# Two multiplications by the reciprocal softmax sums, moved from behind the attention visit to later points of the slot

## The chip, the cores and the metric

The kernel runs on one core of a Trainium2 chip. The metric is the device time of one execution in microseconds (us); less is better. Before the change it is 1352.66 us, the median of three runs (1352.47 to 1352.69).

Names of engines: PE is TensorE (matmuls; PEld are its weight loads), DVE is VectorE, ACT is ScalarE, POOL is GpSimd, SP is SyncE, whose queue issues the DMAs.

## What is computed

An attention with normalised queries and keys, followed by a two-layer network. Cut to what matters (8 batches, 12 heads, 448 positions, 64 elements a head; 768 features, 2048 hidden ones; float32 throughout, the two weights as float64 words):

```python
q_n = q / np.sqrt(np.mean(q * q, axis=-1, keepdims=True) + 1e-06) * g_q      # k_n in the same way, with g_k
scores = np.matmul(q_n, k_n.transpose(0, 1, 3, 2)) / np.sqrt(64)
attn = np.exp(scores - np.max(scores, axis=-1, keepdims=True))
attn = attn / (np.sum(attn, axis=-1, keepdims=True) + 1e-09)
x = np.matmul(attn, v).transpose(0, 2, 1, 3).reshape(8 * 448, 768)
h = x @ w_in
out = (h - np.tanh(h)) @ w_out
```

The division by the sum of the exponentials can wait until after the matmul with `v`: the kernel multiplies the result by the sum's reciprocal. The change is about when it does that.

## The kernel before

**Slots and points.** The attention of one batch is done in six *slots*, one for each pair of heads. Slot `s` is batch `b = s // 6`, pair `hp = s % 6`; there are 48. From slot 12 on, `slot(s)` writes one: first the attention's matmuls, then a list `work` of fourteen *points*. The network's matmuls are a generator, `mlp()`. Between two points `run(...)` takes as many matmuls from it as fit in a fifteenth of the slot's time, `gap_ns(s)` times four; a point then issues a few instructions of the attention's preparation for the slots to come. Nobody reorders this later: each engine works through its instructions in the order in which the Python code issues them. The network of earlier batches runs beside the attention of later ones, and after slot 47 it runs alone.

**The visit.** From slot 13 on (`FOLDED`), the attention part is `visit(s, av)`. It interleaves on TensorE the matmuls of the values of slot `s` (L635, and L623 for the last keys) with those of the scores of slot `s + 1` (L569), and takes some 5.7 us in which no matmul of the network runs. The values go to two banks of PSUM. Then comes `divide(s, av)`: ScalarE copies the first bank to a tile `xT` (L757), VectorE adds the second one (L758), and VectorE multiplies each half of the tile's rows by `rs`, the reciprocal of the sums (two instructions at L762, 64 rows by 448 elements each). After it TensorE computes the third block of the next slot's scores, and then the network goes on.

**The points of a slot**, in order: 1 to 3 add up the next slot's exponentials (`rows`, L600, L606, twice L613); 4 and 5 transpose and reduce them (L710, L717); 6 scales the queries and keys of slot `s + 2` (L530); 7 gathers sums and squares on ScalarE; 8 and 9 transpose queries and keys and sum squares (L540, L544, L508); 10 makes the sums' reciprocals (`spread_sums`, L733 and L734); 11 and 12 are ScalarE's (`weigh_keys`, `meet_blocks`, then `widen_sums`, L741); 13 turns the widened reciprocals into `rs` of slot `s + 1` (`turn_sums`, L747); 14 is empty.

**The network's products.** The hidden layer works by a Strassen-like scheme: seven products in the order 1, 5, 6, 2, 3, 7, 4 (`ORDER`). Each is a chain of matmuls into one of three PSUM banks; products 2, 3 and 7 add to the banks of 1, 5 and 6. After a product VectorE or ScalarE takes the bank's content (an *eviction*: L908 to L924 and L889 for the hidden layer, L1133, L1217, L1223 and L1140 in `project_pair` for the output layer), and the third product after wants the same bank again. In the hidden layer a product is six matmuls, a slot seven products; in `project_pair` a product is four matmuls, and each block of seven is followed by one of eight matmuls of 448 columns (L1126). A matmul of float32 shows as two records.

**x differences.** The Strassen scheme needs differences of x: `x_sums(b, c, ...)` has GpSimd make four of them (L793, 128x224) from the tiles of pairs `c` and `c + 3`. For `c = 0` that is at the fifth point of the slot of pair 4, for `c = 1` at its tenth point, for `c = 2` at the second point of the slot of pair 5. GpSimd also makes the differences of the output layer (`inner_sum`, `u`, L1083), the subtraction of the tanh (L889), and a power for the norms (L523, some 4.8 us, issued by `power_blocks` right behind a visit).

Of the kernel before, what the change touches and what calls it, by code (L numbers as in the profile page):

```python
# [13 lines left out]
ALU = mybir.AluOpType  # L14
# [132 lines left out]
def bounded_path(tc, ctx, q, k, v, moe_w_in, moe_w_out, out, g_col, ident, ones, half_ones, neg_half, early):  # L147
# [17 lines left out]
    nc = tc.nc  # L165
    B, H, S, D = q.shape
# [3 lines left out]
    NP = H // 2  # L170
# [340 lines left out]
    def meet_blocks(s):  # L511

        mine, other = normed["rr", s]
        for g in range(P // BL):
            nc.scalar.copy(out=other[g * BL : (g + 1) * BL], in_=mine[(g ^ 1) * BL : ((g ^ 1) + 1) * BL])
# [32 lines left out]
    def weigh_keys(s):  # L548
        kT = turned[s][1]
        nc.scalar.mul(kT, kT, g_col)  # L550

    def sc_bank():
        return bank_of("sc")

    def scores(s, c, apart=False):

        rr, kT, qT = turned[s]
        n = S if c < KF else HS
        name, bufs = ("p", 2) if c < 2 else ("p_full", 1) if c < KF else ("p_last", 2)
        if c == 1:  # L560
            p = probs[s, 1] = probs[s, 0]
        else:
            p = probs[s, c] = pp.tile([P, 2, 2 if c < 2 else 1, n], F32, name=name, bufs=bufs)
        tiles = [sc_bank() for _ in range(2)]

        def score(h, i):
            at, first = (i * BL, 0) if c < KF else (i * BL % KR, i * BL // KR * n)
            r = slice(h * D, (h + 1) * D)
            nc.tensor.matmul(  # L569
                tiles[h][i * BL : (i + 1) * BL, :n], lhsT=kT[r, c * P + at : c * P + at + BL],  # L570
                rhs=qT[r, first : first + n], start=True, stop=True,
            )

        def exp(h):
            nc.scalar.activation(  # L575
                p[:, h, c if c < 2 else 0, :], tiles[h][:, :n], AF.Exp,
                scale=1.0 if rr is None else rr[:, 0, 2 * c + h : 2 * c + h + 1],
            )

        if apart:  # L580
            return [(lambda i, h=h: score(h, i), lambda h=h: exp(h)) for h in range(2)]
        for i in range(P // BL):
            for h in range(2):
                score(h, i)
        for h in range(2):
            exp(h)
# [5 lines left out]
    def add(s, now=True):  # L592

        if s <= NP + NP // 2:
            sums[s] = []
            return
        t = early["sum"]
        sums[s] = [t]
        p = full(s)
        nc.vector.tensor_tensor(out=t, in0=p[0], in1=p[1], op=ALU.add)  # L600
        if now:
            add_third(s)
# [126 lines left out]
    def spread_sums(s):  # L729

        acc = whole[s]
        total = whole[s] = late["blocks"].tile([2 * BL, NJ], F32, name="sum_all")
        nc.vector.reduce_sum(total, acc.rearrange("p g j -> p j g"), axis=AX.X)  # L733
        nc.vector.reciprocal(total, total)  # L734

    def widen_sums(s):

        total = whole[s]
        room = late["blocks"].tile([P, 2 * S], F32, name="sum_T")
        wide = whole[s] = room[: 2 * BL, :S].rearrange("p (j k) -> p j k", k=BL)  # L740
        nc.scalar.copy(out=wide, in_=total[:, :, None].to_broadcast([2 * BL, NJ, BL]))  # L741
# [7 lines left out]
    def divide(s, av):  # L749
        b, hp = steps[s]  # L750
        rs = whole.pop(s)
        if b > PAIRED and b % 2 and hp == 1:
            x = xT[b, hp] = late["blocks"].tile([P, S], F32, name="xT_more", bufs=1)
        else:
            x = xT[b, hp] = xp.tile([P, S], F32, name="xT")
        if s >= FOLDED:
            nc.scalar.copy(out=x, in_=av[0][:, :S])  # L757
            nc.vector.tensor_tensor(out=x, in0=x, in1=av[1][:, :S], op=ALU.add)  # L758
        for m in range(2):
            rows = slice(m * D, (m + 1) * D)  # L760
            if s >= FOLDED:
                nc.vector.tensor_tensor(out=x[rows], in0=x[rows], in1=rs, op=ALU.mult)  # L762
                continue
            for n in range(2):
                nc.vector.tensor_tensor(
                    out=x[rows, n * HS : (n + 1) * HS], in0=av[n][rows, :HS], in1=rs[n * D : (n + 1) * D],
                    op=ALU.mult,
                )
        for c in range(NCH):
            del probs[s, c]  # L770
        if b < PAIRED and hp >= HC:
            c = hp - HC
            x_sums(b, (c,), range(4), nc.vector if b == 0 and c == HC - 1 else nc.gpsimd)

    def x_sums_later(s, second):
        b, hp = steps[s]
        for c in {(HC + 1, 1): (0,), (HC + 1, 2): (1,), (HC + 2, 0): (2,)}.get((hp, second), ()):
            x_sums(b, (c,), range(4), nc.gpsimd)

    def x_sums(b, chunks, which, eng):  # L780

        for c in chunks:
            x11, x12, x21, x22 = (xT[b, r][:, n : n + HS] for r in (c, c + HC) for n in (0, HS))
            for i in which:
                if i != 2 and (b, i) not in tt:
                    tt[b, i] = tp.tile([P, HC, HS], F32, name=f"tt{i}", bufs=1)
                out, a, z = (
                    lambda: (tt[b, 0][:, c], x12, x11),
                    lambda: (tt[b, 1][:, c], x22, tt[b, 0][:, c]),
                    lambda: (x12, x22, x12),  # L790
                    lambda: (tt[b, 3][:, c], x21, tt[b, 1][:, c]),
                )[i]()
                eng.tensor_tensor(out=out, in0=a, in1=z, op=ALU.subtract)  # L793


    late = {}
# [579 lines left out]
    def gap_ns(s):  # L1376

        if s < 2 * NP:
            return H_NS / 12 if s % NP < 3 else 4 * S / ENGINE_NS * CD * CF / 12
        if s < 3 * NP:  # L1380
            return (H_NS + O_NS + AHEAD_NS) / (4 * NP)
        n = (s - 3 * NP) % (2 * NP)
        return (H_NS / 16, OUTER_NS * SOON / 8, H_NS / 16, OUTER_NS * (len(OUTER) - SOON) / 8)[(n > 3) + (n > 5) + (n > 9)]

    def has(s):
        return 0 <= s < NS

    def first_slot(s):
# [31 lines left out]
        if has(s):  # L1420
            divide(s, av)
# [34 lines left out]
    def slot(s):  # L1456

        gap = gap_ns(s)
        av = av_banks
        if has(s + 1):  # L1460
            scores(s + 1, KF)
        if s < FOLDED:
            last_values(s, av)
            totals(s, sc_bank())
            divide(s, values(s, av))
            for c in range(KF):
                scores(s + 1, c)
        else:
            visit(s, av)
        if has(s + 2):  # L1470
            load(s + 2, "v")
        rows, ahead, following = has(s + 2), has(s + 3), has(s + 1)
        folded = following and s + 1 >= FOLDED
        first = s + 3 == TURNED
        scaled = rows and not first
        if scaled:
            power_blocks(s + 2)
        work = (
            (
                (following, lambda: add(s + 1, False)), (first, lambda: turn(s + 2, sc_bank(), sc_bank())),  # L1480
                (ahead and not first, lambda: load_blocks(s + 3)),
            ),
            (
                (following, lambda: add_third(s + 1)), (first, lambda: load_blocks(s + 3)),
                (True, lambda: x_sums_later(s, 0)),
            ),
            ((following, lambda: add_last(s + 1)),),
            ((folded, lambda: fold(s + 1)),),
            ((folded, lambda: fold_rest(s + 1)), (True, lambda: x_sums_later(s, 1))),
            ((scaled, lambda: scale_blocks(s + 2)),),  # L1490
            ((folded, lambda: gather(s + 1, 0)), (ahead, lambda: square_blocks(s + 3))),
            ((scaled, lambda: turn_blocks(s + 2, 0)), (folded, lambda: gather(s + 1, 1))),
            ((scaled, lambda: turn_blocks(s + 2, 1)), (ahead, lambda: norm_blocks(s + 3))),
            ((folded, lambda: spread_sums(s + 1)), (True, lambda: x_sums_later(s, 2))),
            ((scaled, lambda: weigh_keys(s + 2)), (ahead, lambda: meet_blocks(s + 3))),
            ((folded, lambda: widen_sums(s + 1)),),
            ((folded, lambda: turn_sums(s + 1)),),
            (),
        )
        for point in work:  # L1500
            run(4 * gap / (len(work) + 1))
            for wanted, fn in point:
                if wanted:
                    fn()
        run(4 * gap / (len(work) + 1))
# [10 lines left out]
    for s in range(2 * NP, NS):  # L1516
        slot(s)
# [346 lines left out]
```

## Time and profile before

| what | value |
|---|---|
| median of the three runs | 1352.66 us |
| the profiled execution | 1352.3 us |
| its span, first to last instruction | 1350.5 us |
| TensorE's mean granted clock | 0.997 |
| busy: PE, PEld | 1317.8, 1032.7 us |
| busy: DVE, ACT, POOL | 952.5, 566.3, 772.5 us |
| L762, x 64 (and 6 to `xT_more`) | median 619 ns, at most 1595 ns |
| L758, x 32 (and 3 to `xT_more`) | median 621 ns |
| L793 on POOL | median 659 ns, at most 1507 ns |

The share of busy time is an average over stages that differ: up to about 300 us the weights are converted, from there to about 1190 us attention and network run side by side, and then the network runs alone. "Idle before, releaser" is the time an engine stood still before an instruction, and what ended it. The chain of waits is followed back from the last instruction: at each step to whatever released it.

### The profile page before, as it was taken

What the parts mean: (1) busy time and instruction counts of PE and PEld (TensorE: products, weight loads), DVE (VectorE), ACT (ScalarE), POOL (GpSimd) and SP (SyncE); (2) the same over time, 40 slices, a digit from 0 to 9 for tenths busy, and PEclk for the clock granted to TensorE, in tenths of its full rate; (3) what the DMA queues carried; (4) which work ended last, traced back from release to release, by engine and by line L of the source; (5) the groups of instructions that cost most, each with busy time, mean ns of one, the idle gap of its engine ahead of it and who ended that gap; (6) DMA issues with size and microseconds to landing.
All of it is one profiled execution on the core that took longest, in us unless ns stands there. A gap on an engine that the chain in (4) does not pass through costs nothing.

```text
span 1350.5 us, 29252 instructions
## 1 busy us (share of the span) xinstructions
PE 1317.8 (98%) x11352; PEld 1032.7 (76%) x11352; DVE 952.5 (71%) x1401; ACT 566.3 (42%) x1342; POOL 772.5 (57%) x591
## 2 busy tenths in 40 slices
PE   7988999999999999999999999999999999999997
PEld 3467854478998888687788787778777788689986
DVE  4999978766855667587877576768787667533455
ACT  7856654244433454445322346354612254311102
POOL 4766766347846246726698244934599243812661
PEclk9999999999999999999999999999999999999999
DMA  7879879889999766476655867475745765355545
GB/s 172 193 202 267 257 253 252 245 251 282 333 303 269 178 160 175 114 185 149 174 145 136 201 160 177 122 170 163 180 126 150 151 200 158 115 151 175 172 141 102
DMA packets 364743, 253.53 MB, mean 188 GB/s; under 512 B 273012, under 2 KB 303284, under 8 KB 364596
## 3 DMA queue, kind: packets, MB, share of 16 engines
q1 hardware_dynamic: 364592, 251.57, 68.8%
q8 instruction: 92, 1.51, 0.5%
q14 instruction: 55, 0.45, 0.1%
q10 hardware_dynamic: 4, 0.00, 0.0%
HBM read 205.23 MB, written 46.27 MB: 186 GB/s over the span
## 4 chain that ended last, share of the span: by engine, by line
PE 81%; DVE 9%; SPq 3%; DMA 2%; issue 2%; POOL 2%; ACT 0%; DVEq 0%; ACTq 0%; POOLq 0%
PE mm L841 36%; PE mm L1126 23%; PE sc L569 8%; PE sc L635 6%; PE mm L1319 5%; DVE xT L762 1%; DVE rows L613 1%; PE sc L623 1%; DMA gT<-in_moe_w_in_dram 1%; PE sc L673 1%; SPq L289 1%; SPq L127 1%; POOL u L1083 1%; DVE rows L606 1%; DMA w_raw<-in_moe_w_in_dram 1%
## 5 line engine op out<-in xcount | busy, mean ns | idle before, releaser
L841 PE MATMUL mm<-xT,w_f 128*128 128x224 f32 x1296 | 264.0, 353 | 0.6 <-DVE s L912 0.6
L841 PEld LDWEIGHTS mm<-xT,w_f 128*128 128x128 f32 x1296 | 244.5, 190 | 6.3 <-issue 4.1
L569 PE MATMUL sc<-qT,kT 64*32 64x448 f32 (+1 forms) x3072 | 212.7, 498 | 2.3 <-ACT p_last L575 1.3
L841 PE MATMUL mm<-tt,w_f 128*128 128x224 f32 x1044 | 213.6, 356 | 0.6
L841 PEld LDWEIGHTS mm<-tt,w_f 128*128 128x128 f32 x1044 | 195.0, 190 | 18.6 <-issue 15.4
L523 POOL TENSOR_TENSOR rr_mine<-rr_mine,neg_half 128x28 f32<-128x28 f32 x33 | 160.5, 4864 | 2.8
L758 DVE TENSOR_TENSOR xT<-xT,sc 128x448 f32<-128x448 f32 x32 | 19.9, 621 | 178.1 <-PE sc L569 124.1
L1126 PE MATMUL mm<-u,w_f 128*128 128x224 f32 x672 | 136.6, 354 | 1.3 <-DVE sum_all L733 0.9
L889 POOL TENSOR_TENSOR gT<-s,th 128x448 f32<-128x448 f32 x44 | 55.8, 1271 | 142.4 <-ACT th L888 142.4
L1126 PE MATMUL mm<-gT,w_f 128*128 128x224 f32 (+1 forms) x496 | 133.0, 420 | 3.2 <-DVE acc L1133 2.8
L1126 PEld LDWEIGHTS mm<-u,w_f 128*128 128x128 f32 x672 | 126.0, 190 | 8.5 <-POOL u L1083 3.8
L569 PEld LDWEIGHTS sc<-qT,kT 64*32 64x32 f32 x3072 | 70.5, 106 | 69.0 <-issue 51.6
L1126 PEld LDWEIGHTS mm<-gT,w_f 128*128 128x128 f32 x496 | 93.3, 190 | 38.1 <-issue 31.8
L635 PE MATMUL sc<-p,v_nat 64*32 64x448 f32 x1120 | 110.5, 536 | 0.0
L725 ACT COPY sum_g<-sum 32x14 f32<-32x14 f32 x280 | 56.3, 201 | 106.0 <-DVE sum L717 100.3
L1126 PE MATMUL mm<-g,w_f 128*128 128x224 f32 (+1 forms) x360 | 99.5, 428 | 0.0
L575 ACT ACTIVATE p<-sc 128x448 f32<-128x448 f32 x132 | 71.8, 544 | 50.6 <-PE sc L569 36.5
L889 POOL TENSOR_TENSOR g<-s,th 128x448 f32<-128x448 f32 x24 | 30.7, 1280 | 108.2 <-ACT th L888 93.2
L1126 PEld LDWEIGHTS mm<-g,w_f 128*128 128x128 f32 x360 | 67.9, 190 | 27.1 <-issue 26.0
L1319 PE MATMUL mm<-gT,w_out 128*128 128x448 f32 x192 | 74.3, 542 | 0.0
L1083 POOL TENSOR_TENSOR u<-gT 128x448 f32<-128x448 f32 x48 | 59.5, 1260 | 11.1 <-PE mm L1126 11.1
L635 PEld LDWEIGHTS sc<-p,v_nat 64*32 64x32 f32 x1120 | 40.6, 107 | 31.1 <-issue 31.1
(203 smaller groups left out, 2450.0 us busy)
## 6 DMA issues: line engine op xcount, KB each, us to landing
w_f<-w_in SPq DMA_DIRECT2D x196, 384.0 KB, 3.5
w_f<-w_inner SPq DMA_DIRECT2D x63, 512.0 KB, 3.7
w_f<-w_out SPq DMA_DIRECT2D x42, 512.0 KB, 3.9
w_raw<-in_moe_w_out_dram SPq DMA_DIRECT2D x16, 768.0 KB, 5.3
w_in<-w_out SPq DMA_DIRECT2D x21, 384.0 KB, 5.2
qk_nat<-in_q_dram SPq DMA_DIRECT2D x132, 56.0 KB, 2.6
qk_nat<-in_k_dram SPq DMA_DIRECT2D x132, 56.0 KB, 2.3
g<-w_out SPq DMA_DIRECT2D x14, 512.0 KB, 5.4
```

Of the source, the lines that this page charges most:

```text
L127: nc.sync.dma_start(out=last[r * KR : (r + 1) * KR], in_=rest.rearrange("h p d -> p h d"))
L523: nc.gpsimd.tensor_tensor(out=mine, in0=mine, in1=neg_half[:, :1].to_broadcast([P, 2 * NJ]), op=ALU.pow)
L569: nc.tensor.matmul(tiles[h][i * BL : (i + 1) * BL, :n], lhsT=kT[r, c * P + at : c * P + at + BL], rhs=qT[r, first : first + n], start=True ...
L575: nc.scalar.activation(p[:, h, c if c < 2 else 0, :], tiles[h][:, :n], AF.Exp, scale=1.0 if rr is None else rr[:, 0, 2 * c + h : 2 * c + h ...
L635: nc.tensor.matmul(av[g][i * BL : (i + 1) * BL, :S], lhsT=v_nat[keys, h, c, m * BL : (m + 1) * BL], rhs=p[keys, h], start=first, stop=True ...
L725: nc.scalar.copy(out=acc[h * BL : (h + 1) * BL, g], in_=part[g * BL : (g + 1) * BL, h * NJ : (h + 1) * NJ])
L758: nc.vector.tensor_tensor(out=x, in0=x, in1=av[1][:, :S], op=ALU.add)
L841: nc.tensor.matmul(bank[:, f * HS : (f + 1) * HS], lhsT=w[:, c * width + f, :], rhs=moving[p](c), start=(first and f == 0 and c == 0), sto ...
L889: eng.tensor_tensor(out=g[:, rows, cols], in0=h, in1=th, op=ALU.subtract)
L1083: nc.gpsimd.tensor_tensor(out=u[:, half], in0=a[:, half], in1=z[:, half], op=ALU.subtract)
L1126: nc.tensor.matmul(bank[:, :n], lhsT=w(i), rhs=mv, start=(first and i == 0), stop=(i == len(moving) - 1), skip_group_check=not first,)
L1319: nc.tensor.matmul(bank[:, :S], lhsT=w_out_row(f, n // HC)[:, n % HC * P : (n % HC + 1) * P], rhs=g[:, f, :], start=(f == 0), stop=(f == C ...
```

## The change

Three things in the folded slots (13 to 47). The two multiplications are no longer issued behind the add in `divide`; they are put on a list, and the eleventh and the twelfth point issue one each. In a batch's last slot (`hp == 5`) they stay where they were. The differences of `c = 1` go from the tenth point to the fourteenth.

```diff
         if s >= FOLDED:
             nc.scalar.copy(out=x, in_=av[0][:, :S])
             nc.vector.tensor_tensor(out=x, in0=x, in1=av[1][:, :S], op=ALU.add)
+            for m in range(2):
+                rows = x[m * D : (m + 1) * D]
+                late.setdefault("divide", []).append(
+                    lambda rows=rows: nc.vector.tensor_tensor(out=rows, in0=rows, in1=rs, op=ALU.mult)
+                )
         for m in range(2):
             rows = slice(m * D, (m + 1) * D)
             if s >= FOLDED:
-                nc.vector.tensor_tensor(out=x[rows], in0=x[rows], in1=rs, op=ALU.mult)
+                if hp == NP - 1:
+                    divide_rows()
                 continue
...
+    def divide_rows():
+        if late.get("divide"):
+            late["divide"].pop(0)()
...
-            ((folded, lambda: spread_sums(s + 1)), (True, lambda: x_sums_later(s, 2))),
-            ((scaled, lambda: weigh_keys(s + 2)), (ahead, lambda: meet_blocks(s + 3))),
-            ((folded, lambda: widen_sums(s + 1)),),
+            ((folded, lambda: spread_sums(s + 1)),),
+            (
+                (scaled, lambda: weigh_keys(s + 2)), (ahead, lambda: meet_blocks(s + 3)),
+                (True, divide_rows),
+            ),
+            ((folded, lambda: widen_sums(s + 1)), (True, divide_rows)),
             ((folded, lambda: turn_sums(s + 1)),),
-            (),
+            ((True, lambda: x_sums_later(s, 2)),),
```

## The prediction

> **What bounds the kernel now.** I read the page first, then the chain of waits by stretches, then VectorE's and TensorE's timelines around single visits. The page's first part and its chain:
>
> ```profile
> PE 1317.8 (98%) x11352; PEld 1032.7 (76%) x11352; DVE 952.5 (71%) x1401; ACT 566.3 (42%) x1342; POOL 772.5 (57%) x591
> PE 81%; DVE 9%; SPq 3%; DMA 2%; issue 2%; POOL 2%; ACT 0%; DVEq 0%; ACTq 0%; POOLq 0%
> ```
>
> TensorE sets the time, yet 9% of the chain is VectorE, and L762, the line that the change moves, has a share of it. The 98% hides short stops, because a matmul record (352 ns) is longer than the distance from one start to the next (190 ns, the weight load's length). So I looked for starts further apart than that. The slot that begins at 1159 us (number 46 = batch 7, pair 4; s = 6 x batch + pair) has the worst of them. Its TensorE timeline (start, length, then in brackets the idle time before it and who ended it):
>
> ```profile
> 1159.20 1.78 PE L1126 MATMUL mm<-u,w_f 128*128 128x224 f32 x8
> 1160.82 1.68 PE L1126 MATMUL mm<-gT,w_f 128*128 128x224 f32 x8
> 1163.20 1.78 PE L1126 MATMUL mm<-gT,w_f 128*128 128x224 f32 x8 [0.71 <-DVE acc L1133]
> 1165.11 3.27 PE L1126 MATMUL mm<-u,w_f 128*128 128x224 f32 x16
> 1170.08 7.23 PE L1126 MATMUL mm<-gT,w_f 128*128 128x448 f32 x21 [1.70 <-DVE acc L1133]
> ```
>
> TensorE stops for evictions (L1133), and the chain of waits over the same stretch shows why they are late:
>
> ```profile
> 1159.30 0.63 DVE xT L758
> 1159.93 0.02 issue
> 1159.95 1.30 DVE xT L762
> 1161.25 0.03 issue
> 1161.28 1.44 DVE xT L762
> 1162.73 0.03 issue
> 1162.76 0.39 DVE acc L1133
> 1163.15 1.52 DVE rows L600
> ...
> 1169.75 0.29 DVE acc L1133
> 1170.04 0.04 issue
> 1170.08 9.31 PE mm L1126 x32
> ```
>
> VectorE waits for the visit's last matmuls, then adds (L758), multiplies twice (L762), and only then reaches the eviction of a product finished before or during the visit. From there it has no pause until TensorE has stopped three times.
>
> The slots without a stop have a fixed length: L758 starts at 757.77, 779.24 and 800.73, 21.5 us apart. Slot 26 takes 22.64 (617.95 to 640.59). I summed, slot by slot, the part of each start-to-start distance over 0.19 us (0.38 for 448 columns), less the two gaps of 0.09 and 0.10 at a visit's ends that every slot has. In us: s20 0.42, s22 0.87, s23 0.29, s26 1.07, s27 0.69, s28 0.65, s32 0.53, s34 0.86, s35 0.35, s38 1.07, s39 0.64, s40 0.64, s44 0.50, s46 3.30; nothing in the others from s13 on. Together 11.9 us, and every one ends with an eviction by VectorE that comes late in an unbroken row of VectorE work since the visit.
>
> **What the Trainium skill says.** "VectorE: DVE Perf Modes", section on the TRN2 errata, gives an fp32 tensor_tensor (N+151)/0.96 ns: 624 ns for 448 elements. The trace's median for L762 is 619, so it agrees. "SBUF — State Buffer", section "Who interferes with whom", says that a VectorE instruction with two SBUF inputs contends with a GpSimd one that reads SBUF, and the later one blocks. L762 has two SBUF inputs, and the trace agrees in direction: 1.30 and 1.44 us at 1159.95, with GpSimd in its differences (L1083), against 0.62 in quiet slots. "PSUM — Partial Sum Buffer", section "PSUM bank collisions raise a hardware error", tells one to guard a bank by semaphore; here TensorE restarts at 1170.08, 0.05 us after the eviction's end. "Perfetto Trace Analysis", section "Tensor Engine Instruction (MATMUL, LD_WEIGHTS)", says that VectorE is strictly first in, first out, and the whole argument rests on that order.
>
> **The change, part by part.** 35 visits are folded ones (s13 to s47). Six are a batch's last (s17, 23, 29, 35, 41, 47) and keep their place; 29 visits move 58 multiplications. Nothing is added or removed: VectorE's 952.5 us stay, and the instructions moved issue no DMA.
>
> *Taken from behind the visit.* Every VectorE instruction from the visit to the eleventh point comes earlier by 2 x 0.62 = 1.24 us where GpSimd is quiet, by 2.1 (s22, s28) to 2.8 (s46) where it isn't. Where GpSimd is streaming, L600 is next to meet it (1.09 free, 1.60 in s46), so part of the excess comes back there. I count on 1.24 at least less 0.5 of such a shift, 1.24 as the likely value, 2.8 at most. All the sums above but s46's are under 1.24, so they go: 11.24 us in the twelve slots that move (the list without s23 and s35). In s46 I follow the row: without L762, L1133 at 1159.9, L600 to 1161.9, L1133 to 1162.2, L606 (1.7) and L613 (2.0) to 1165.9, transpose to 1167.0, L1133 to 1167.4. TensorE, not stopped before, wants the bank at 1159.3 + 5 x 1.52 = 1166.9; about 0.5 stays. Gain **10.7** of 11.24.
>
> *Put at the eleventh point.* VectorE's order there is row sum and reciprocal (L733, L734), then the first multiplication, then the eviction of product 4 (L924), then the second one, then L747. In slot 27, the one furthest behind, L924 runs at 655.76 and ends at 656.31. It now starts 1.24 earlier and behind one multiplication more, 0.62 to 1.45: between 0.6 earlier and 0.2 later. TensorE writes that bank again three products on (1, 5, then 6), after the visit, at 662.68. That spare of 6.4 us is the cover; without it the price is up to 1.24 us in each of the 20 slots of this kind (s18 to 21, 24 to 27, 30 to 33, 36 to 39, 42 to 45). Cost **0**.
>
> *Put at the twelfth point.* Behind it stands L747, whose result is wanted behind the next visit, or much later now; VectorE idles 3.9 to 8.1 us before L758. Before L747 it also waits 0.2 to 1.2 us for ScalarE's L741, which the second multiplication fills. Cost 0, except in the long slots s28 and s40. There the points are 2.74 us apart. By counting matmuls from gap_ns, the eleventh falls after the first matmul of a product 1, in front of the 1.19 us that VectorE idles before 693.83: free. The twelfth falls at the end of product 5, in front of its eviction (698.17 to 698.55), whose bank TensorE wants at 699.68. Free (0.62) it fits; contended (1.3 to 1.45, and GpSimd streams differences until 701.2) TensorE loses 0.2 to 0.4. I take 0.3 each: **0.6** back.
>
> *The x differences last.* Four GpSimd subtractions (0.66 each, 3.8 us for the four with contention in s28) move from the tenth point to the fourteenth, in six slots. They now follow the multiplication they need by two points, so the wait is met. In s28 and s40 GpSimd does them at 701.15, ten us late already; they now let two inner sums (four L1083) past, which helps those sums if anything. Still ahead of the power that the next slot issues, nothing there is later. Their reader, the next hidden layer, begins at 749. Cost 0; if the cover were gone, 3.8 us in each of the two.
>
> *SP's queue, ScalarE, TensorE's own order.* No instruction of theirs moves. What is late next after VectorE: GpSimd in s27/28, s39/40 and s46 (24.4 us busy of the 25 from 1150), but none of the stops traced back ends with it.
>
> Sum: 10.7 - 0.6 = 10.1. Against the profiled execution: 1352.3 (span 1350.5 and 1.8 around it) becomes 1342.2. The median of the runs is 0.36 above the profiled one: **1342.6**.
>
> **The rivals.** *The lag falls by less.* GpSimd's contention passes whole to L600 and L606, and the row is 0.72 us earlier only (1.24 less 0.52). Then each slot gains the smaller of its sum and 0.72: 7.7, less 1.5 for contended multiplications: 6.2, time 1346.5. For it: L600 took 1.60 and L606 1.72 in s46. Against: in s20 and s32 L600 took its free 1.09 after a slowed L762.
> *GpSimd takes the place of VectorE.* Its sums keep TensorE where it was in s27, 28, 39, 40 and s46; gains stay in s20, 22, 26, 32, 34, 38, 44: 5.3, time 1347.3. For it: GpSimd's busy time there. Against: its sums of 1159.64 to 1165.6 are for the next block.
> *Nothing is gained*, because the stops follow something that moves with the visit; or the order that the compiled program gets is not the one the source says: 1352.
> *Slower.* The eviction of product 4 behind the first multiplication sets TensorE back in the 20 hidden slots, 1.24 each: 24.8 less 11.2 is 13.6, time 1366. It decides from where VectorE reaches that eviction over 6.4 us later than now, or where the bank's next matmul comes before the visit; the records put it after.
>
> **How the numbers follow.** Forecast 0.62, smaller lag 0.14, GpSimd 0.09, no change 0.05, slower 0.10. Less than 0.2% (2.7 us) can't be told from no change. Faster 0.85, same 0.05, slower 0.10. The range goes from all 11.24 us and a little contention saved (1341.0) to beyond the GpSimd case (1348.5); the two last cases, 0.15, are left out.
>
> **What would show it.** Right: TensorE's gaps behind L1133, L912 and L889 gone in the twelve slots, s26 21.5 us long, s23 and s35 as they were; L600 directly behind the add; VectorE's share of the chain lower by about the 1% of L762. The one new gap, if any, is in s28 and s40 before product 3. Wrong: gaps at the same places (the row is not the cause), gaps before a visit (the tail is), or TensorE waiting for L1083.

## The result, and the profile after

Six runs of the changed kernel took 1346.34 us in the median (1344.73 to 1349.41), six of the kernel before 1352.57 (1352.17 to 1352.90). The ratio is 0.9955 with a 95% interval of 0.9945 to 0.9966: 6.2 us less, where 10 were forecast. The profiled execution took 1346.23 us, with a span of 1344.4. Behind the edit all lines stand ten further down: L1133 is now L1143, L1083 is L1093, L889 is L899. The page's first part and its chain:

```profile
PE 1315.8 (98%) x11352; PEld 1035.4 (77%) x11352; DVE 967.6 (72%) x1401; ACT 570.0 (42%) x1342; POOL 789.3 (59%) x591
PE 82%; DVE 5%; POOL 4%; SPq 3%; DMA 3%; issue 2%; ACT 1%; ACTq 0%; DVEq 0%; POOLq 0%
```

(SPq is SP's queue; "issue" is time in which an engine waited for nothing that the profile shows.) VectorE's share of the chain fell from 9% to 5%, where the prediction expected about one point less, and GpSimd's rose from 2% to 4%. Their instruction counts are the same, yet VectorE is busy 15 us longer and GpSimd 17. Single instructions of both take longer where the two work side by side, as the lines below show.

Slot 46 shows what was hoped for and what was left. TensorE's timeline (start, length, and in brackets the idle time and its releaser):

```profile
1155.32 1.78 PE L1136 MATMUL mm<-u,w_f 128*128 128x224 f32 x8
1156.94 3.19 PE L1136 MATMUL mm<-gT,w_f 128*128 128x224 f32 x16
1159.96 3.19 PE L1136 MATMUL mm<-u,w_f 128*128 128x224 f32 x16
1164.10 7.79 PE L1136 MATMUL mm<-gT,w_f 128*128 128x448 f32 x24 [0.94 <-DVE acc L1143]
```

and the chain of waits over it:

```profile
1155.42 0.62 DVE xT L758
1156.04 0.30 DVE acc L1143
1156.34 1.39 DVE rows L600
...
1157.95 1.73 DVE rows L606
1159.68 0.02 issue
1159.71 1.44 DVE rows L613
1161.14 0.03 issue
1161.17 1.46 DVE rows L613
1162.63 0.02 issue
1162.66 1.11 DVE sum_T L710
1163.77 0.29 DVE acc L1143
1164.06 0.04 issue
1164.10 5.91 PE mm L1136 x15
```

The eviction now follows the add at once, and of three stops one is left. The row up to it is shorter by the two multiplications, but what is left of it is slower than it was: L613 takes 1.44 and 1.46 us. In the kernel before it took 0.96 and 0.98:

```profile
1166.64 0.96 DVE rows L613
1167.63 0.98 DVE rows L613
```

It now runs beside GpSimd's differences of the output layer (L1093, 128x448; below they are called inner sums); before, it ran beside the smaller x differences (L793, 128x224). In the quiet slot 30 the two halves take 1.27 us together.

In a slot like 26, where the stops went altogether, L600 follows the add directly:

```profile
617.43 0.62 DVE L758 TENSOR_TENSOR xT<-xT,sc 128x448 f32<-128x448 f32 x1 [3.56 <-PE sc L569]
617.97 1.08 DVE L600 TENSOR_TENSOR rows<-p 128x896 f32<-128x896 f32 x1
```

I took the stops from the distances of TensorE's starts, in the way of the prediction. One table holds the kernel before, the changed one and the experiments told below (us, one profiled execution each, slots with a stop over 0.1 in the first two; "none" leaves the 58 multiplications out, "both" has them in both places, "x last" moves the differences alone, "last" treats the last slots too, "weights" has the other order of loads, "best" puts three edits together):

| slot | before | changed | none | both | x last | last | weights | best |
|---|---|---|---|---|---|---|---|---|
| 20 | 0.42 | 0 | 0 | 0.55 | 0.44 | 0 | 0 | 0 |
| 22 | 0.87 | 0 | 0 | 1.19 | 0.87 | 0 | 0 | 0 |
| 23 | 0.29 | 0.47 | 0.74 | 0.30 | 0.30 | 0 | 0.46 | 0 |
| 26 | 1.07 | 0 | 0 | 1.07 | 1.07 | 0 | 0 | 0 |
| 27 | 0.69 | 0 | 0 | 0.70 | 0.70 | 0 | 0 | 0 |
| 28 | 0.65 | 0.52 | 0 | 1.14 | 0.65 | 0.53 | 0.54 | 0.54 |
| 29 | 0 | 0.45 | 0 | 0.46 | 0 | 0 | 0.46 | 0 |
| 30 | 0 | 0.88 | 0 | 0.76 | 0 | 0.88 | 0 | 0 |
| 32 | 0.53 | 0 | 0 | 0.49 | 0.53 | 0 | 0 | 0 |
| 34 | 0.86 | 0 | 0 | 1.12 | 0.87 | 0 | 0 | 0 |
| 35 | 0.35 | 0.45 | 0.71 | 0.48 | 0.35 | 0 | 0.47 | 0 |
| 38 | 1.07 | 0 | 0 | 1.17 | 1.07 | 0 | 0 | 0 |
| 39 | 0.64 | 0 | 0 | 0.64 | 0.64 | 0 | 0 | 0 |
| 40 | 0.64 | 0.52 | 0 | 1.15 | 0.66 | 0.53 | 0.53 | 0.53 |
| 41 | 0 | 0.46 | 0 | 0.63 | 0 | 0 | 0.47 | 0 |
| 42 | 0 | 0.38 | 0.47 | 0 | 0 | 1.18 | 0 | 0 |
| 44 | 0.50 | 0 | 0 | 0.46 | 0.49 | 0 | 0 | 0 |
| 46 | 3.31 | 1.21 | 1.05 | 5.17 | 3.32 | 1.21 | 1.22 | 0 |
| sum | 11.9 | 5.3 | 3.0 | 17.5 | 12.0 | 4.3 | 4.2 | 1.1 |

From before to changed the sum falls by 6.5 us; the two profiled executions differ by 6.1, and the changed one reached the first visit 0.6 us later (L758 at 307.09, not 306.49), where the code is the same. So the table accounts for the result: the old stops went in nine of the twelve slots, three kept a part or got another one in its place, and four slots that had none have one now.

### The profile page after: what moved, and what is told of

Read it like the earlier page. It is cut to its first block, busy times and chain, and to the rows that moved or that the text cites. A ratio compares the mean times of both kernels' runs of the same rounds, so it can differ in the third digit from the quotient of the medians.

```text
span 1344.4 us, 29274 instructions
## 1 busy us (share of the span) xinstructions
PE 1315.8 (98%) x11352; PEld 1035.4 (77%) x11352; DVE 967.6 (72%) x1401; ACT 570.0 (42%) x1342; POOL 789.3 (59%) x591
## 4 chain that ended last, share of the span: by engine, by line
PE 82%; DVE 5%; POOL 4%; SPq 3%; DMA 3%; issue 2%; ACT 1%; ACTq 0%; DVEq 0%; POOLq 0%
PE mm L851 38%; PE mm L1136 20%; PE sc L569 8%; PE mm L1329 5%; PE sc L635 5%; POOL u L1093 2%; PE sc L673 1%; PE sc L623 1%; POOL rr_mine L523 1%; SPq L965 1%; PE mm L673 1%; SPq L127 1%; DMA w_f<-w_inner 1%; SPq L497 1%; DMA qk_nat<-in_k_dram 1%
## 5 line engine op out<-in xcount | busy, mean ns | idle before, releaser
L758 DVE TENSOR_TENSOR xT<-xT,sc 128x448 f32<-128x448 f32 x32 | 19.9, 621 | 165.1 <-PE sc L569 115.8
L899 POOL TENSOR_TENSOR gT<-s,th 128x448 f32<-128x448 f32 x44 | 57.5, 1308 | 138.0 <-ACT th L898 138.0
L575 ACT ACTIVATE p<-sc 128x448 f32<-128x448 f32 x132 | 71.7, 543 | 50.4 <-PE sc L569 36.0
L899 POOL TENSOR_TENSOR g<-s,th 128x448 f32<-128x448 f32 x24 | 30.3, 1263 | 104.1 <-ACT th L898 104.1
L1093 POOL TENSOR_TENSOR u<-gT 128x448 f32<-128x448 f32 x48 | 63.5, 1344 | 11.1 <-PE mm L1136 11.1
L144 POOL TENSOR_TENSOR rr<-rr,neg_half 112x8 f32<-112x8 f32 (+1 forms) x30 | 49.1, 1664 | 26.7 <-DVE rr L143 26.1
```

Of the source, the lines that this page charges most:

```text
L144: nc.gpsimd.tensor_tensor(out=r, in0=r, in1=neg_half[:rows], op=ALU.pow)
L575: nc.scalar.activation(p[:, h, c if c < 2 else 0, :], tiles[h][:, :n], AF.Exp, scale=1.0 if rr is None else rr[:, 0, 2 * c + h : 2 * c + h ...
L899: eng.tensor_tensor(out=g[:, rows, cols], in0=h, in1=th, op=ALU.subtract)
L1093: nc.gpsimd.tensor_tensor(out=u[:, half], in0=a[:, half], in1=z[:, half], op=ALU.subtract)
```

## The experiments

**The differences alone.** Is anything of this due to the third edit? The kernel before, with that edit only:

```diff
-            ((folded, lambda: spread_sums(s + 1)), (True, lambda: x_sums_later(s, 2))),
+            ((folded, lambda: spread_sums(s + 1)),),
...
-            (),
+            ((True, lambda: x_sums_later(s, 2)),),
```

> Only the x differences go from the tenth to the fourteenth point; the multiplications stay behind the visit. Theory A (the whole gain is VectorE's row behind the visit getting shorter, the differences carry nothing): 1352.6 us, within 1 us of before, TensorE's stops in slots 20, 22, 26, 27, 32, 34, 38, 39, 44 as in before, 0.4 to 1.1 us each. Rival B (the differences' move brings the new stops of slots 28 to 30 and 40 to 42, because GpSimd's sums come in another order against VectorE): these stops, 3.2 us in all, appear here too, with the old ones still there, time 1354 to 1356.

1353.00 against 1352.92, ratio 0.9999 (0.9991 to 1.0008), and the stops of before in every slot (one more, of 0.68 in slot 17, where nothing of the edit is, is not in the table). Moved alone, the differences carry nothing; theory A holds. What their new place does together with the late multiplications was not run.

**Neither place.** What would be left if the multiplications cost nothing anywhere?

```diff
     def divide_rows():
-        if late.get("divide"):
-            late["divide"].pop(0)()
+        fn = late["divide"].pop(0) if late.get("divide") else None
+        return fn
...
                 if hp == NP - 1:
-                    divide_rows()
+                    divide_rows()()
```

> The changed kernel without the 58 multiplications of the 29 slots (the division by the sums is left out there), x differences at the fourteenth point. Theory A (the new stops of slots 28 to 30, 40 to 42 and 46 are other work that stands next in line: GpSimd's sums, SP's queue, the rest of VectorE's row in slot 46): those stops stay, most of them within 0.3 us, and the time is 1345 to 1346.5, as the changed kernel's 1346.3. Rival C (the multiplications cost TensorE 3 to 4 us at their new points): the stops go with them, time about 1342.5.

1344.11 (1342.88 to 1350.19), ratio 0.9945 (0.9929 to 0.9961), which lies between the two theories. The stops of slots 28, 29, 30, 40 and 41 went with the multiplications, against theory A; those of 23, 35, 42 and 46 did not, against rival C. In stops, the new points cost 5.3 - 3.0 = 2.3 us, not the 0.6 of the prediction.

**Both places.** What if the multiplications stand in the old place and in the new one?

```diff
                 if hp == NP - 1:
                     divide_rows()
+                else:
+                    nc.vector.tensor_tensor(out=x[rows], in0=x[rows], in1=rs, op=ALU.mult)
```

> The 58 multiplications stand behind the visit and again at the eleventh and twelfth point (those rows are multiplied by the reciprocal twice). Theory A (the place behind the visit costs 10 us of stops, the later points cost nothing): time of before, 1352.5 within 1 us, with the stops of before. Rival C (the later points cost 3 to 4 us): 1355.5 to 1357, with stops that before does not have, late in the slots.

1357.66 against 1352.92, ratio 1.0036 (1.0023 to 1.0049): 4.7 us over the kernel before. Rival C's time is the nearer one (0.7 above its range), and A's is out; but the stops that were added do not lie late in the slots, as C said: they lie in the row behind the visit (slots 22, 28, 34, 40, 46), in the last slots 29 and 41, and in slot 30. The place behind the visit costs 12.2 us (17.5 less 5.3) with the later one filled, and 8.9 (11.9 less 3.0) without it. The later points cost 5.6 on top of the row behind the visit, and 2.3 alone. Some 1.7 of the 5.6 is a second effect of one long stop: in slot 46 TensorE stood 2.53 us from one start to the next, and then began its next matmuls of 448 columns 0.75 us apart, not 0.38, until 1177.3 us, at a granted clock of 0.51 by the profile. After the 2.06 us of the kernel before the clock stayed at 1.00. The prediction's cost of 0 for the later points comes nearly true in the slots of the hidden layer's first three pairs (18 to 20, 24 to 26 and so on; slot 30 has a cause of its own, told below), and not where GpSimd is busy.

**Which of the new points cost?** One kernel leaves out the multiplications of slots 27 and 39, the other those of 28 and 40. Each ran once (1346.63 and 1343.34 us), so only their traces are read:

```diff
+        if s in (27, 39):
+            late["divide"].clear()
         for m in range(2):
```

> The changed kernel without the four multiplications of slots 27 and 39 (the division is left out for these two pairs of heads). Theory G (these, late in a slot in which GpSimd makes its subtractions and sums, slow GpSimd's unbroken row, and TensorE pays in the middle of the next slot): the stops of slots 28 and 40, 0.52 us each, fall to under 0.1; those of slots 29 and 41 (0.45) stay or fall with them. Rival H (the stop in slot 28 comes from TensorE arriving earlier, whatever the multiplications do): 0.52 stays.

> The changed kernel without the four multiplications of slots 28 and 40 (the division is left out for these two). Theory G: the stops of slots 29 and 41 (0.45 us each), where VectorE's multiplications behind the visit took 2.97 instead of 2.09 us because GpSimd is later, go or fall under 0.1; those of 28 and 40 stay at 0.52, since they come before the eleventh point. Rival H (slot 29's stop is inherited from slot 28's): it stays.

The stops of slots 29 and 41 went in both runs, as theory G says: slot 29 stops only if both sets are there. In slots 28 and 40 a stop of the same size stayed (0.49 us in the first kernel, 0.53 in the second), and by its size H is right. But its place says otherwise. In the changed kernel TensorE stops for GpSimd's inner sums, in the middle of slot 28:

```profile
681.64 2.43 PE L1136 MATMUL mm<-u,w_f 128*128 128x224 f32 x12
684.33 1.02 PE L1136 MATMUL mm<-u,w_f 128*128 128x224 f32 x4 [0.26 <-POOL u L1093]
```

With the multiplications of slot 27 left out, it doesn't stop there but 14 us later, for VectorE. First VectorE's timeline of that kernel (its lines are two further down), then TensorE's:

```profile
694.55 2.02 DVE L1086 TENSOR_TENSOR gT<-gT,g 128x896 f32<-128x896 f32 x1
696.60 1.44 DVE L762 TENSOR_TENSOR xT<-xT,rs_T 64x448 f32<-64x448 f32 x1
698.07 0.69 DVE L1145 TENSOR_TENSOR s<-mm,s 128x224 f32<-128x224 f32 x2
```

```profile
696.62 1.68 PE L1138 MATMUL mm<-g,w_f 128*128 128x224 f32 x8
698.52 1.78 PE L1138 MATMUL mm<-g,w_f 128*128 128x224 f32 x8 [0.23 <-DVE s L1145]
```

This is the stop that the prediction had named: the second multiplication, slowed to 1.44 us, in front of product 5's eviction, and TensorE late at product 3 (0.39 us and 0.10 behind it). In the changed kernel it doesn't show: there TensorE has lost as much already in front of it, and the same multiplication takes the same 1.44 us. Two limits stand side by side in these slots, each worth 0.5 us, and each covers the other: with either set of multiplications left out the other limit's stop is there, and the kernel without any of the 58 is rid of both. The GpSimd one begins in slot 27: there the late multiplications meet GpSimd's subtraction (1.32 us, 1.14 without them), its inner sums come later, and so does the power behind them. GpSimd's lines in the changed kernel, then in the one without the multiplications (the visit's add starts at 660.49 and at 659.73):

```profile
665.70 5.58 POOL L523 TENSOR_TENSOR rr_mine<-rr_mine,neg_half 128x28 f32<-128x28 f32 x1
680.36 3.92 POOL L1093 TENSOR_TENSOR u<-g,u 128x448 f32<-128x448 f32 x2
```

```profile
664.46 4.81 POOL L523 TENSOR_TENSOR rr_mine<-rr_mine,neg_half 128x28 f32<-128x28 f32 x1
677.49 3.92 POOL L1093 TENSOR_TENSOR u<-g,u 128x448 f32<-128x448 f32 x2
```

By the inner sum that TensorE wants (it ends at 684.28, and at 681.41) GpSimd is 2.1 us later against the add.

**The last slots too.** Slots 23, 29, 35 and 41 keep the multiplications behind the visit. Here they go to the seventh and eighth point, the third differences to the ninth:

```diff
             if s >= FOLDED:
-                if hp == NP - 1:
-                    divide_rows()
                 continue
...
-        for c in {(HC + 1, 1): (0,), (HC + 1, 2): (1,), (HC + 2, 0): (2,)}.get((hp, second), ()):
+        for c in {(HC + 1, 1): (0,), (HC + 1, 2): (1,), (HC + 2, 3): (2,)}.get((hp, second), ()):
...
-            ((folded, lambda: gather(s + 1, 0)), (ahead, lambda: square_blocks(s + 3))),
-            ((scaled, lambda: turn_blocks(s + 2, 0)), (folded, lambda: gather(s + 1, 1))),
-            ((scaled, lambda: turn_blocks(s + 2, 1)), (ahead, lambda: norm_blocks(s + 3))),
+            ((folded, lambda: gather(s + 1, 0)), (ahead, lambda: square_blocks(s + 3)), (s % NP == NP - 1, divide_rows)),
+            ((scaled, lambda: turn_blocks(s + 2, 0)), (folded, lambda: gather(s + 1, 1)), (s % NP == NP - 1, divide_rows)),
+            ((scaled, lambda: turn_blocks(s + 2, 1)), (ahead, lambda: norm_blocks(s + 3)), (True, lambda: x_sums_later(s, 3))),
```

> The changed kernel, and in a batch's last slot the multiplications go to the seventh and eighth point and the third differences to the ninth. Theory A (VectorE's row behind the visit makes the stops of slots 23, 29, 35 and 41 too, 0.45 to 0.47 us each): these four go, 1.84 us less than the changed kernel, 1344.5. Rival D (in slots 29 and 41 GpSimd or SP's queue stands next in line, so that the gain there turns into a longer stop in slots 30 and 42): only 0.9 us less, 1345.4, and the stops of slots 30 and 42 grow by about 0.45 each.

1344.92, ratio 0.9947 (0.9935 to 0.9959), 1.4 us under the changed kernel; the interval overlaps the changed kernel's, so the traces decide here. All four stops went, as A says, and slot 42's grew from 0.38 to 1.18, while slot 30's stayed: rival D in one of the two. The stop of slot 29 was a row behind the visit as well: in the changed kernel the two multiplications there take 2.97 us, and took 2.09 before. The lines of the changed kernel, then that of the kernel before:

```profile
708.79 2.97 DVE L762 TENSOR_TENSOR xT<-xT,rs_T 64x448 f32<-64x448 f32 x2
711.79 1.91 DVE L600 TENSOR_TENSOR rows<-p 128x896 f32<-128x896 f32 x1
```

```profile
711.20 2.09 DVE L762 TENSOR_TENSOR xT<-xT,rs_T 64x448 f32<-64x448 f32 x2
```

GpSimd, late from slot 28, ends its inner sums 6.6 us behind the add there, and before 5.7. In both kernels the multiplications run beside them, so the delay fits, but how it makes the multiplications that much longer was not shown.

**The weights in slots 30 and 42.** The stops of slots 30 and 42 end with a DMA, `w_f<-w_in`, not with an engine. SP's timeline of the changed kernel (each row the issues of one kind; lengths are the time to issue):

```profile
748.97 3.48 SPq L965 DMA_DIRECT2D out_dram<-acc  x4
752.55 0.44 SPq L426 DMA_DIRECT2D w_f<-w_in  x1
753.09 2.12 SPq L965 DMA_DIRECT2D out_dram<-acc  x4
755.26 1.03 SPq L117 DMA_DIRECT2D v_nat<-in_v_dram  x2
756.34 2.54 SPq L127 DMA_DIRECT2D v_nat<-in_v_dram  x2
758.93 2.15 SPq L497 DMA_DIRECT2D qk_nat<-in_q_dram  x4
761.13 2.04 SPq L497 DMA_DIRECT2D qk_nat<-in_k_dram  x4
763.27 3.61 SPq L426 DMA_DIRECT2D w_f<-w_in  x6
```

SP issues without a pause, stores and loads of mostly half a microsecond each, and the weights of product 4 (763.27) wait behind eight loads of queries and keys. What counts is the distance from the visit's add to that issue. Over the two slots of six kernels it was 6.13, 6.32, 6.41, 6.66, 6.76 and 6.78 us where there was no stop, and 7.31, 7.32, 7.45, 7.46, 7.74 and 7.96 us where there was one (0.38, 0.47, 0.88, 0.76, 0.88, 1.18). The two single runs fit it too: 0.03 us at 6.94, and 0.33, 0.45 and 0.87 us at 7.45, 7.59 and 7.70. The kernel before stood at 6.66 and 6.32, with little to spare. First I moved the value loads that these slots issue (for slots 32 and 44) to ScalarE's queue; `fetch` takes the queue as a new argument (not shown):

```diff
-                fetch(nc, name, t, src[b, 2 * hp : 2 * hp + 2], in_order(s))
+                fetch(nc, name, t, src[b, 2 * hp : 2 * hp + 2], in_order(s), nc.scalar if s in (32, 44) else None)
```

> The changed kernel; the value loads that slots 30 and 42 issue (four DMAs each) go through ScalarE's queue and not SP's. Theory S (in these slots the network's weights come late because SP's queue is full with issues): the weights are issued some 3.5 us earlier, the stops of slots 30 (0.88) and 42 (0.38) go, time 1.3 us under the changed kernel's, 1345.0. Rival T (the DMA engines themselves are the limit): the stops stay, time unchanged.

1363.11, ratio 1.0071 (1.0057 to 1.0085): the losses in these two slots grew to 8.1 us each, which neither theory had. Of these, some 1.4 us in slot 30 and 1.7 in slot 42 are again matmuls at half the usual rate behind the longest stop. SP's queue stood still for ten us in the middle of its stores. Below are SP's wait from 744 to 760 us (in total, how often, the longest), the stores, and the first moved load on ScalarE's queue:

```profile
SPq L965 <- DMA v_nat<-in_v_dram: 10.2, 1, 10.2
```

```profile
746.44 12.13 SPq L965 DMA_DIRECT2D out_dram<-acc  x4
755.90 0.54 ACT L575 ACTIVATE p_full<-sc 128x448 f32<-128x448 f32 x1
755.95 0.40 ACTq L117 DMA_DIRECT2D v_nat<-in_v_dram  x1
```

The kept trace tells why a store waits for loads of another queue. Each DMA tells of its landing by a semaphore. From 300 us on, the program takes eight semaphores in turn for the DMAs of both queues (in the changed kernel's trace every one of 890 steps goes to the next of the eight), and in 912 pairs whose landing is recorded no DMA is issued before the one ahead of it on its semaphore has landed. The store that stood from 748.04 to 758.26 has the semaphore of the first moved load. On ScalarE's queue that load was issued only at 755.95, between two of its exponentials (L575). A later store started at 762.18, when the fourth moved load, on its semaphore, had landed at 762.16; in slot 42 a store started at 1078.43, the load on its semaphore having landed at 1078.42, and that wait took 8.6 us. So the move tied SP's queue to the point that ScalarE had reached. The run says nothing against theory S and doesn't prove it. So the order was changed instead:

```diff
-                (ahead and not first, lambda: load_blocks(s + 3)),
+                (ahead and not first and s not in (30, 42), lambda: load_blocks(s + 3)),
...
-                (following, lambda: add_third(s + 1)), (first, lambda: load_blocks(s + 3)),
+                (following, lambda: add_third(s + 1)), (ahead and (first or s in (30, 42)), lambda: load_blocks(s + 3)),
```

> The changed kernel; in slots 30 and 42 the loads of queries and keys (eight DMAs on SP's queue) are issued at the second point and not at the first, so that the weights of product 4 are issued before them. Theory S (the stops of slots 30 and 42 are the weights' issue coming 7.3 us and more behind the visit's add, since SP's queue is busy with issues): the weights are issued some 4 us earlier, the stops of 0.88 and 0.38 go, 1345.0 against 1346.3. Rival T (the queries and keys, 0.5 us later, then hold up ScalarE's squares and with them evictions): as long a stop elsewhere in these slots, time unchanged.

1344.92 (1344.25 to 1345.37), ratio 0.9941 (0.9928 to 0.9955), and both stops are gone, with no new one in these slots. The interval touches the changed kernel's; it is the trace that tells the two apart. SP's timeline of this kernel:

```profile
755.71 2.56 SPq L127 DMA_DIRECT2D v_nat<-in_v_dram  x2
758.37 0.54 SPq L426 DMA_DIRECT2D w_f<-w_in  x1
758.95 1.99 SPq L497 DMA_DIRECT2D qk_nat<-in_q_dram  x4
```

Theory S holds: the first of these weights is issued 3.2 and 2.5 us behind the add.

**Together.** A first kernel had the last slots, the value loads on ScalarE's queue, and in slot 46 the last addition, transpose and reduction two points later:

```diff
+        if s == NS - 2:
+            work = list(work)
+            work[2:7] = (), (), work[2], work[3], work[4] + work[6]
```

> The multiplications of a batch's last slots moved too, the value loads of slots 30 and 42 on ScalarE's queue, and in slot 46 the last addition of the exponentials, the transpose and the reduction two points later. If each stop is what it was traced to: slots 23, 29, 35, 41 none, 30 and 42 none, slot 46 from 1.3 to under 0.3, slots 28 and 40 still 0.52: 3.2 us under the kernel with the last slots moved (1344.9), so 1341.7. If SP's queue or VectorE's row is only one of two that stand in line: 1343 to 1344.5.

1360.07, ratio 1.0044 (1.0030 to 1.0058), because of the two long stops (9.3 and 7.1 us) in slots 30 and 42; the stops of slots 46, 23, 29, 35 and 41 went, as expected. With the other order of loads in place of ScalarE's queue:

> The multiplications of the last slots moved too, the weights before queries and keys in slots 30 and 42, and in slot 46 the last addition, transpose and reduction two points later. If the causes are as traced and don't cover one another: stops left only in slots 28 and 40 (0.52 each) and 0.1 in slot 46, 1341.7. If moving them frees a limit behind: up to 1343.5.

1341.92 (1340.97 to 1342.81), ratio 0.9919 (0.9906 to 0.9933). The table's last column is what was expected: 0.54 and 0.53 left in slots 28 and 40, and none in 46. Its interval lies clear below the changed kernel's, and the stops add up: their causes don't cover one another, but for the pair in slots 28 and 40.

## Why the prediction was right, and where its sizes were off

*The row behind the visit* was right, slot by slot: every old stop of slots 20, 22, 26, 27, 32, 34, 38, 39 and 44 went, also the late ones of 27 and 39 just before the next visit. Slot 26 takes 21.57 us now, as long as those without a stop. The gain of 10.7 that the prediction counted for this place is 10.0 of 11.2 in the table (all but slot 46's 1.2; what slots 28 and 40 show now is another stop), and by the stops of all slots the place is worth 8.9 ("before" less "none") or 12.2 ("both" less "changed"), so the way from the multiplications to TensorE's stops is shown. What failed is the count of what stands behind it.

The sum of 10.1 us lost 3.6 in five terms (stops, from the table):

- *Slot 46*, "about 0.5 stays": 1.2 stayed (1.11 up to the eviction and 0.10 behind it). The step took L606 and the two halves of L613 at the lengths they had in the old place, 1.7 and 2.0; L606 kept its 1.7, and beside GpSimd's inner sums the two halves of L613 took 2.9. The rule of the Trainium skill that the prediction used for L762 ("SBUF — State Buffer", section "Who interferes with whom": an instruction of VectorE with two SBUF inputs contends with one of GpSimd that reads SBUF) holds for L613 as well, as 1.44 and 1.46 against 0.63 in a quiet slot show, and I had not carried it on down the row. The page's lock, with the later one blocked, does not describe the lengths: here both sides stretch, GpSimd's L1093 to 1.7 us each, where it takes 1.1 with VectorE idle (at 1152.31). Off by 0.7.
- *The twelfth point in slots 28 and 40*, "I take 0.3 each": 0.49 where it could be seen, and the 0.52 in the changed kernel is GpSimd's, which covers it. Off by 0.4, and by a cause that the sum did not have.
- *Slots 29 and 41*, not in the sum at all: 0.45 and 0.46. The step "what is late next after VectorE" named GpSimd and put it at nothing, since no old stop ended with it. But the multiplications at the late points make GpSimd's row longer, and VectorE's row behind the next visit with it: without those of slots 27 and 39, or of 28 and 40, these two stops are gone. Off by 0.9.
- *Slots 30 and 42*: 0.88 and 0.38. "SP's queue ... No instruction of theirs moves" was true and not enough. SP's queue was full in this stretch and its weights came just in time: the distance from add to issue was 6.66 and 6.32 us before, 7.45 and 7.31 in the changed kernel. It differs from trace to trace (6.13 in slot 30 of "none", 7.32 in slot 42 of the same). Off by 1.3.
- *Slots 23 and 35*, "as they were": 0.18 and 0.10 more. They are VectorE's row, since they go when the multiplications there move; why they grew is open, and not by the late multiplications, since in "none" they are 0.74 and 0.71. Off by 0.3.

The measured 1346.3 is almost the 1346.5 of the rival *the lag falls by less*, but that is chance: by it slots 22, 26, 34 and 38 would have kept 0.14 to 0.35 us each and slot 46 2.6, and the table shows 0 and 1.2. Of the other rivals, that of GpSimd was right in kind for slots 28 and 40, where the prediction's sign of being wrong, TensorE waiting for L1083 (now L1093), did appear, at 0.5 us each; but it also had slots 27 and 39, in which TensorE stayed free. The slower rival did not come: no stop appeared in front of a visit, so the cover for product 4's eviction held.

## What to carry to other kernels

When an engine that feeds the bottleneck is relieved, list for every queue behind it how much spare it has at that place, not only whether it has ended a wait: SP's weights had ended none, and had a few tenths of a microsecond of spare (an estimate from the distances above: 6.66 and 6.32 before, and the first stops from 7.3 on). A piece of work moved to a "free" point is free only if it meets nobody there; look at what the neighbour that the engine contends with is doing at that time. And two limits side by side hide one another: leave one out and look where the stop is, not only how long. Before DMAs are given to another queue, look which semaphores they share with the ones that stay: here the move cost more than the change had gained.

## What the runs showed of the hardware that was not expected

A stop of TensorE can cost more than its length. After 2.53 us without a start in slot 46 of the kernel with both places, and after 4.51 and 5.68 us in the kernel with ScalarE's queue, its matmuls started at half the usual rate for some 3 to 4 us (0.75 us apart for 448 columns, 0.37 for 224), at a granted clock of 0.50 to 0.51 by the profile; after 2.06 us in the kernel before they did not.

And the busy time of unchanged instructions is no constant: with the same 1401 and 591 instructions VectorE was busy 967.6 us, not 952.5, and GpSimd 789.3, not 772.5. A half of L613 took 0.63 us in slot 30, where GpSimd stood still, 0.96 and 0.98 beside the x differences and 1.44 and 1.46 beside the inner sums.
